# Attention, MoE and MLP in one static plan: the port of SBUF in the planner, routing on GpSimd, weight residues on VectorE, and the first pair split out of PSUM in pieces

## The chip, the cores and the metric

One core of a Trainium2 chip. The metric is the device time of one execution in microseconds (us), the median of the runs. Engines are named as in the profile: PE is TensorE (PEld its weight loads), DVE is VectorE, ACT is ScalarE, POOL is GpSimd, SP is SyncE, which here only issues DMAs.

## The reference

```python
def reference(q, k, v, moe_*, moe2_*):        # all float32
    x = attention(q, k, v)                    # [4, 8, 576, 64], block causal mask (blocks of 64), softmax
    x = x.transpose(0, 2, 1, 3).reshape(2304, 512)
    logits = x @ w_gate                       # 8 experts
    noisy = logits + log1p(exp(x @ w_noise)) * noise
    # top 2 of 8 per token, softmax over the two
    x = sum_k top2_w[k] * (relu(x @ w1[e_k]) @ w2[e_k])     # w1 [8, 512, 1024], w2 [8, 1024, 512]
    h = x @ w_in                              # [512, 2048]
    return (h * clip(h + 3, 0, 6) / 6) @ w_out
```

## The kernel before

Every large product is made of three: each operand is split into a high part (rounded to fp32r) and a low part (the residue), and hi*hi, hi*lo and lo*hi are summed in PSUM. So each operand costs a cast and a subtraction on some engine besides its load.

**Attention** works through 16 pairs of heads, four pairs to a batch. For a pair, TensorE transposes q and k (`prep`), the result goes to SBUF (`prep_out`: `qs`, `ks`) and is split into `qd` and `kt` (`q_hi`, `q_lo`, `k_hi`, `k_lo`); `qd` holds the two heads side by side with zeros between, set once by memsets. Six score units (`scores`) fill the PSUM tiles `sb`; VectorE takes the row maximum (`rowmax`), ScalarE the exponential (`expo`), TensorE transposes P (`ptrans`), which is split again (`pt_hi`, `pt_lo`), then come P times v (`av`), and a product with `iw` (`fin`) that turns the heads' outputs back and adds their share of the router's logits. `lsum` adds up the logits of a batch's four pairs, `lgm` brings them into token order.

**Routing** (`route`) of a batch is a chain of some fifty small instructions: softplus, the noisy logits, the top two (`top`, `ti`), one-hots (`oh`, `ohb`), positions by a triangular product (`pos`), and the lists of token ids by a product of ten one-hot selections (`sel`) with two tables (`rid`), `idm`. Batches 0 to 2 are routed during attention. After batch 2 two tiles of tokens of expert 0 are gathered early (`early_load`). The last batch is routed after attention, while TensorE computes expert 0 for the two early tiles; then its `ids` allow the gathers of the other three tiles (`load_x`), and the experts and the MLP run in a written-out order to the end.

**The order** of attention and of the hand-over comes from a list scheduler in the kernel's Python, `Plan`. `add(engines with costs, function, deps, priority, take, drop)` records an operation; `run` walks a model of time, gives each free engine the ready operation of lowest priority number, and emits it. Where an operation lists two engines, the first is preferred. `PR` holds the priorities and choices, found offline; `SELS`, `WLS` and `VHS` are choices that it indexes. `plan` orders attention, `plan2` the hand-over. Each engine executes what is emitted in that order, and waits where an operand is late. TensorE first does WARM0 matmuls on zeros.

In the kernel before: the memsets of `qd` stand on GpSimd (L612); pair 0 goes the way of the other pairs, with its splits on VectorE, ScalarE and GpSimd; all four loads of q and k of the first pairs are issued by SyncE; of the routing GpSimd has most small steps of batch 0 alone (`rp`: 1), the selections are VectorE's in all batches; the residues of expert 0's weights in the hand-over are GpSimd's (`WLS[2]`, L324).

Of the kernel before, what the change touches and what calls it, by code (L numbers as in the profile page):

```python
# [19 lines left out]
WARM0 = 9  # L20
# [12 lines left out]
WLS = ({"DVE": 1.14, "POOL": 2.4}, {"POOL": 2.4, "DVE": 1.14}, {"POOL": 2.4})  # L33
VHS = ({"POOL": 2.3}, {"DVE": 0.42}, {"POOL": 2.3, "DVE": 0.42}, {"DVE": 0.42, "POOL": 2.3}, {"ACT": 0.65, "DVE": 0.42})
PR = {'v': -0.45, 'prep': -10.04, 'step': -0.65, 'qk': -35.17, 'keep': 1, 'S': 0.31, 'max': -27.6, 'exp': -16.28, 'pt': 0.44, 'hi': 17.54, 'lo': -16.57, 'hid': True, 'av': 4.37, 'o': 10.18, 'od': True, 'inv': -4.2, 'fin': 13.84, 'x': -26.38, 'route': 27.64, 'rp': 1, 'route2': 10.65, 'xt': 12, 'eg': 537.67, 'ex': 466.81, 'ew': 2093.4, 'first': 0, 'sel': 2, 'vh': 0, 'wl': 2, 'wa': 8.24, 'wb': 12.71, 'h': -29.8, 's2': 0.04, 'vs': (0.29, -0.33, -1.3, 0.67, -3.03, -2.34), 'vpt': (7.17, 2.34, 0.89, -2.5, -6.05, 0.37, 1.12, 0.7000000000000001), 'vp': (0.79, -0.62), 'vf': (0.46, -1.86)}
# [10 lines left out]
class Plan:  # L46
# [11 lines left out]
    def add(self, eng, fn, deps=(), prio=0.0, take=None, drop=None, lat=None, after=0.0):  # L58
        if drop is not None:
            drop.left += 1  # L60
        self.ops.append((eng, fn, {d for d in deps if d is not None}, prio, take, drop, lat))
        self.ready.append(after)
        return len(self.ops) - 1

    def run(self, start):
# [10 lines left out]
        back = []  # L76
        left = len(ops)
        now = 0.0
        while left:
# [4 lines left out]
            for e in self.LAT:  # L84
# [3 lines left out]
                for i in open_:  # L88
# [13 lines left out]
                eng, fn, _, _, take, drop, lat = ops[i]  # L102
# [6 lines left out]
                free[e] = end  # L109
                done = end + (self.LAT[e] if lat is None else lat)  # L110
# [21 lines left out]
def kernel(  # L132
# [51 lines left out]
    def load(p, nm):  # L184
# [4 lines left out]
        for i in range(2):  # L189
            nc.sync.dma_start(t[:, 0:NC - 1, i], hs[i, 0:S - BLK, :].rearrange("(c p) d -> p c d", p=128))  # L190
        nc.sync.dma_start(t[:BLK, NC - 1], hs[:, S - BLK:, :].rearrange("h p d -> p h d"))

    for nm in "qk":
        nc.vector.memset(raw[nm, 0][64:, NC - 1], 0.0)
        load(0, nm)
# [154 lines left out]
    def early(shape, nm):  # L350
        return e_p.tile(shape, F32R, name=nm)
# [50 lines left out]
    def route(b, dep, add, bank, psum, prio0, after=0.0):  # L402
# [12 lines left out]
        def step(nm, eng, fn, *deps, **kw):  # L415
            prio[0] += 0.25
            dp[nm] = add(eng, fn, [dp[d] for d in deps] if deps else dep, prio[0], after=after, **kw)
# [3 lines left out]
        po = {"POOL": 0.3} if b < PR["rp"] else dv  # L421
# [770 lines left out]
    k2 = {}  # L1192
# [178 lines left out]
```

## Time and profile before

| | |
|---|---|
| median of 3 runs | 1132.49 us (1131.97 to 1132.53) |
| the profiled execution | 1132.54 us, of it 1130.8 us span |
| busy: TensorE, VectorE, ScalarE, GpSimd | 1106.3, 767.4, 525.9, 315.0 us |
| mean granted clock of TensorE | 0.987 |

TensorE's row of 40 slices (28 us each), in tenths: 7 in the first, 9 in nearly all others, 8 in the last. The granted clock is 7 in the first slice and 9 (90% or more) elsewhere. A granted clock of 1.00 is 2.4 GHz, 0.50 is 1.2 GHz; a mean between the two mixes stretches of both.

### The profile page before, as it was taken

How to read it: one execution, taken by the hardware profiler on the slowest of the kernel's cores; microseconds unless marked ns; L12 is line 12 of the kernel's file. 1: busy time of each engine (PE TensorE's matmuls, PEld its weight loads, DVE VectorE, ACT ScalarE, POOL GpSimd, SP SyncE). 2: the span in 40 equal slices, each digit the busy share in tenths (PEclk: the TensorE clock that was granted, in tenths of full speed). 3: DMA queues.
4: the chain of work that ended last, by engine and by line, in shares of the span. 5: the costliest groups of instructions: out<-in, count | busy, mean ns of one | idle time of the engine just before them, and what ended most of it. 6: DMA issues, size and time to landing. Idle time of an engine off the chain costs nothing. (4 is left out here: it accounts for less than half of the span.)

```text
span 1130.8 us, 17329 instructions
## 1 busy us (share of the span) xinstructions
PE 1106.3 (98%) x6426; PEld 981.4 (87%) x6426; DVE 767.4 (68%) x1432; ACT 525.9 (47%) x1074; POOL 315.0 (28%) x333
## 2 busy tenths in 40 slices
PE   7999999998999999999999999999999999999998
PEld 6999989897889999999999989898888888888886
DVE  6777897887577877887887865687554655554542
ACT  4877767653433333333333334565444444344442
POOL 7677776627401010101010000266220320200000
PEclk7999999998999999999999999999999999999999
DMA  5555442120977667567446323412101110000000
GB/s 121 140 125 125 91 104 64 23 60 15 334 271 274 213 236 268 205 225 241 164 165 219 136 101 111 152 47 75 47 28 38 46 30 38 19 1 1 38 1 38
DMA packets 141152, 130.82 MB, mean 116 GB/s; under 512 B 85768, under 2 KB 106248, under 8 KB 141064
## 3 DMA queue, kind: packets, MB, share of 16 engines
q1 hardware_dynamic: 127784, 100.30, 28.6%
q0 software_dynamic: 6080, 19.93, 6.0%
q10 hardware_dynamic: 7200, 9.44, 2.4%
q8 instruction: 52, 0.85, 0.3%
q14 instruction: 36, 0.29, 0.1%
HBM read 92.94 MB, written 36.70 MB: 115 GB/s over the span
## 5 line engine op out<-in xcount | busy, mean ns | idle before, releaser
L366 PE MATMUL h<-xh,wah 128*128 128x312 f32 (+5 forms) x832 | 280.5, 337 | 1.8 <-ACT xh L340 0.7
L367 PE MATMUL h<-xl,wah 128*128 128x312 f32 (+5 forms) x832 | 275.5, 331 | 0.3 <-DVE xl L345 0.3
L368 PE MATMUL h<-xh,wal 128*128 128x312 f32 (+5 forms) x832 | 275.4, 331 | 0.0
L1007 PE MATMUL y<-wbh,hh 128*128 128x512 f32 (+1 forms) x608 | 238.5, 392 | 2.2 <-issue 2.2
L1008 PE MATMUL y<-wbl,hh 128*128 128x512 f32 (+1 forms) x608 | 239.0, 393 | 0.0
L1009 PE MATMUL y<-wbh,hl 128*128 128x512 f32 (+1 forms) x608 | 238.1, 392 | 0.0
L366 PEld LDWEIGHTS h<-xh,wah 128*128 128x128 f32 x832 | 157.9, 190 | 14.4 <-DVE hl L392 0.9
L367 PEld LDWEIGHTS h<-xl,wah 128*128 128x128 f32 x832 | 158.0, 190 | 12.0 <-DVE xl L345 0.5
L368 PEld LDWEIGHTS h<-xh,wal 128*128 128x128 f32 x832 | 157.8, 190 | 10.3
L1009 PEld LDWEIGHTS y<-wbh,hl 128*128 128x128 f32 (+1 forms) x608 | 114.0, 187 | 25.4
L1007 PEld LDWEIGHTS y<-wbh,hh 128*128 128x128 f32 (+1 forms) x608 | 113.9, 187 | 24.1 <-issue 2.6
L1008 PEld LDWEIGHTS y<-wbl,hh 128*128 128x128 f32 (+1 forms) x608 | 113.9, 187 | 21.6
L1300 DVE SCALAR_TENSOR_TENSOR r<-r,h 128x512 f32<-128x512 f32 (+1 forms) x80 | 50.6, 633 | 109.5 <-ACT r L1299 109.2
L389 ACT ACTIVATE hh<-h 128x312 fp32r<-128x312 f32 (+4 forms) x128 | 55.1, 431 | 149.2 <-PE h L368 147.2
L1171 POOL DMA_INDIRECT ga<-y_tab,slot x32 | 37.2, 1162 | 293.4 <-DMA y_tab<-yo 112.1
L985 POOL DMA_INDIRECT xn<-x_tok,ids x38 | 38.5, 1013 | 269.1 <-PE xps L337 266.5
L1299 ACT ACTIVATE r<-h,three 128x512 f32<-128x512 f32 (+1 forms) x80 | 51.6, 645 | 127.5 <-PE h L368 127.4
L324 DVE TENSOR_TENSOR wal<-wa,wah 128x1024 fp32r<-128x1024 f32 x75 | 93.2, 1243 | 14.3 <-ACT wah L320 13.3
L324 DVE TENSOR_TENSOR wbl<-wb,wbh 128x1024 fp32r<-128x1024 f32 x71 | 86.6, 1220 | 13.4 <-ACT wbh L320 10.7
L722 ACT ACTIVATE P<-sb,nm 128x576 f32<-128x576 f32 (+4 forms) x144 | 75.4, 530 | 39.7 <-DVE nm L716 37.0
L320 ACT CAST wbh<-wb 128x1024 fp32r<-128x1024 f32 x80 | 84.0, 1050 | 17.7 <-PE y L1009 16.3
L340 ACT CAST xh<-xps 128x512 fp32r<-128x512 f32 x56 | 32.8, 587 | 127.4 <-PE xps L337 127.4
(246 smaller groups left out, 1871.3 us busy)
## 6 DMA issues: line engine op xcount, KB each, us to landing
wa<-in_moe_w_dram SPq DMA_DIRECT2D x23, 512.0 KB
wb<-in_moe_w_dram SPq DMA_DIRECT2D x23, 512.0 KB
y_tab<-yo SPq DMA_DIRECT2D x32, 256.0 KB
w<-in_moe_w_in_dram SPq DMA_DIRECT2D x16, 512.0 KB
y_tab<-zero SPq DMA_DIRECT2D x8, 1024.0 KB
w<-in_moe_w_out_dram SPq DMA_DIRECT2D x16, 512.0 KB
x_tok<-x SPq DMA_DIRECT2D x32, 144.0 KB
wa<-in_moe_w_dram ACTq DMA_DIRECT2D x9, 512.0 KB
```

The costliest lines, as they stand in the source:

```text
L320: nc.scalar.copy(w_s[which, u][0], raws[PS[u]][which])
L324: (nc.gpsimd if e == "POOL" else nc.vector).tensor_tensor(lo, raws[PS[u]][which], hi.bitcast(F32), op=OP.subtract)
L366: nc.tensor.matmul(ps, lhsT=wh, rhs=xh, start=first, stop=False)
L367: nc.tensor.matmul(ps, lhsT=wh, rhs=xl, start=False, stop=False)
L368: nc.tensor.matmul(ps, lhsT=wl, rhs=xh, start=False, stop=last)
L389: nc.scalar.activation(h[0][:, c0:c1], ps[:, :c1 - c0], AF.Relu)
L722: nc.scalar.activation(o, views.pop((p, i)), AF.Exp, bias=nms.pop((p, i)), scale=1.0, accum_out=rs[p % 3][:, i:i + 1])
L1007: nc.tensor.matmul(yps[t][:n], lhsT=hh[:, sl], rhs=wh[:, f % 2], start=first, stop=False)
L1008: nc.tensor.matmul(yps[t][:n], lhsT=hh[:, sl], rhs=wl[:, f % 2], start=False, stop=False)
L1009: nc.tensor.matmul(yps[t][:n], lhsT=hl[:, sl], rhs=wh[:, f % 2], start=False, stop=last)
L1299: nc.scalar.activation(r[:, :n], ps[:, :n], AF.Relu, bias=three, scale=1.0)
L1300: nc.vector.scalar_tensor_tensor(r[:, :n], r[:, :n], 6.0, ps[:, :n], op0=OP.min, op1=OP.mult)
```

## The change

- `Plan` gets a flag `port` per operation and a record `held`: a flagged operation of VectorE or GpSimd is not placed while the other of the two runs a flagged one. Splits from SBUF, sums of logits and most routing steps are flagged.
- `route`: for batches 0 to 2 all elementwise steps, the tables and the ten selections go to GpSimd (the fused step `nl0` becomes two); for the last batch all go to VectorE.
- Weight residues of expert 0 go to VectorE (`wl`: 0). Two units, (0, 0) and (1, 0), are split during attention (`PRE`), not one.
- Pair 0: k is loaded from ScalarE's queue; q and k are split straight out of PSUM in three pieces (`first_hi`, `first_lo`: blocks 0 to 3, 4 to 7, 8), and a score unit waits only for the pieces that it reads. The `qd` memsets go to VectorE. WARM0 is 6 for 9, and FILL = 8 matmuls on zeros may be placed where TensorE has nothing ready (lowest priority).
- `PR` is new throughout: the order of attention and of the hand-over changes everywhere.

```diff
-WARM0 = 9
+WARM0 = 6
+FILL = 8
+PRE = ((0, 0), (1, 0))
-WLS = ({"DVE": 1.14, "POOL": 2.4}, {"POOL": 2.4, "DVE": 1.14}, {"POOL": 2.4})
+WLS = ({"DVE": 1.2}, {"DVE": 1.14, "POOL": 2.4}, {"POOL": 2.4, "DVE": 1.14}, {"POOL": 2.4})
...
+                    if o[7] and e in other and held[other[e]] > now:
+                        continue
...
+                if port and e in other:
+                    held[e] = end
...
-        load(0, nm)
+        load(0, nm, nc.sync if nm == "q" else nc.scalar)
...
+            port = nm not in ("ez", "lu", "e2", "top", "ti", "pos", "t", "pi", "idm", "id", "os", "cnt", "short")
...
         off = {"DVE": 0.11} if last else {"POOL": 0.24}
-        po = {"POOL": 0.3} if b < PR["rp"] else dv
+        po = off
...
-                step(f"sel{i}{c}", ({"DVE": 0.17, "POOL": 0.6} if last else SELS[PR["sel"]]), lambda e, i=i, c=c: eng_of(e).tensor_scalar(
+                step(f"sel{i}{c}", ({"DVE": 0.17} if last else {"POOL": 0.61}), lambda e, i=i, c=c: eng_of(e).tensor_scalar(
...
-                    nc.gpsimd.memset(t[64 * h:64 * h + 64, :, 1 - h].bitcast(F32), 0.0)
+                    nc.vector.memset(t[64 * h:64 * h + 64, :, 1 - h].bitcast(F32), 0.0)
...
+        FIRST = ((0, 4), (4, 8), (8, NB))
+        def first_hi(e, g, nm, m):
+            src = first_src(g, nm, m)
+            i = slice(*FIRST[m])
+            if nm == "k":
+                copy(e, kt[0][0][:, i.start * BLK:i.stop * BLK], src)
+                return
+            for h in range(2):
+                r = slice(64 * h, 64 * h + 64)
+                scale(e, qd[0][0][r, i, h], src[r].rearrange("p (i s) -> p i s", s=BLK))
+        def first_lo(e, g, nm, m):
...
+            if nm == "k":
...
+                nc.vector.tensor_tensor(kt[0][1][:, c], src, kt[0][0][:, c].bitcast(F32), op=OP.subtract)
+                return
...
+                nc.vector.scalar_tensor_tensor(qd[0][1][r, i, h], src[r].rearrange("p (i s) -> p i s", s=BLK), qscale,
+                                               qd[0][0][r, i, h].bitcast(F32), op0=OP.mult, op1=OP.subtract)
...
+                for n_ in range(FILL):
+                    g = Bank("t", 1)
+                    add({"PE": 0.23}, lambda e, g=g: nc.tensor.matmul(tb[g.bank], lhsT=ones, rhs=filler, start=True, stop=True),
+                        [k["T", 0, 2]], 1e6, take=g, drop=g)
...
+        for n_, (w, u) in enumerate(PRE):
+            hi_ = add({"ACT": 0.95}, lambda e, w=w, u=u: split_hi(w, u, early), [], PR["ew"] + n_, after=205.0)
+            add({"DVE": 1.2}, lambda e, w=w, u=u: split_lo(w, u, e), [hi_], PR["ew"] + n_, port=True)
```

VectorE at the start, between its constants and its first row maxima (`nm<-sb`), before:

```order
L224 COPY iw<-ident 64x4x64 x2
L580 COPY ks<-tb_172 128x512
L580 COPY ks<-tb_173 128x64
L580 CAST qd0h<-qs 64x9x64 x2
L684 TENSOR_TENSOR qd0l<-qs,qd0h 64x9x64 x2
L251 CAST laneb<-lane 128x128
L252 CAST tidi<-tid 128x20
L253 TENSOR_SCALAR tidh<-tidi 128x20
L254 CAST tab<-tidh 128x20
L255 TENSOR_SCALAR tidi<-tidi 128x20
L256 CAST tab<-tidi 128x20
L580 CAST sp_v<-raw_v_77 128x10x64
```

and now:

```order
L234 COPY iw<-ident 64x4x64 x2
L630 MEMSET qd0h 64x9x64 x2
L630 MEMSET qd0l 64x9x64 x2
L630 MEMSET qd1h 64x9x64 x2
L630 MEMSET qd1l 64x9x64 x2
L733 SCALAR_TENSOR_TENSOR qd0l<-tb_171,qd0h 64x4x64 x2
L729 TENSOR_TENSOR kl<-tb_172,kh 128x256
L733 SCALAR_TENSOR_TENSOR qd0l<-tb_171,qd0h 64x4x64 x2
L729 TENSOR_TENSOR kl<-tb_172,kh 128x256
L733 SCALAR_TENSOR_TENSOR qd0l<-tb_173,qd0h 64x64 x2
L729 TENSOR_TENSOR kl<-tb_173,kh 128x64
L765 TENSOR_REDUCE nm<-sb_176 128x1 x3
```

The splits of pair 0 come from PSUM (`tb`) in pieces, behind eight memsets, and the six table operations (`laneb`, `tidi`, `tidh`, `tab`) stand further down. On TensorE, seven of the eight fillers stand between the transposes of pair 0 and its first score.

VectorE in the hand-over, from the copy of the last batch's logits (`lg`) on, before:

```order
L580 COPY lg_154<-tb_173 128x80
L432 TENSOR_SCALAR zc<-lg_154 128x40
L434 TENSOR_SCALAR zx<-lg_154 128x40
L427 TENSOR_TENSOR zx<-zx,noise 128x40
L427 TENSOR_TENSOR zx<-zx,lg_154 128x40
L436 TENSOR_SCALAR u<-ez 128x40
L427 TENSOR_TENSOR en<-ez,noise 128x40
L438 TENSOR_SCALAR dd<-u 128x40
L392 SCALAR_TENSOR_TENSOR hl<-h,hh 128x256
L440 RECIPROCAL rd<-dd 128x40
L427 TENSOR_TENSOR rd<-rd,en 128x40
```

and now (`wal`, `wbl` are the residues of expert 0's weights, `hl` that of its hidden layer):

```order
L598 COPY lg_154<-tb_173 128x80
L334 TENSOR_TENSOR wal<-wa,wah 128x1024
L446 TENSOR_SCALAR zc<-lg_154 128x40
L334 TENSOR_TENSOR wbl<-wb,wbh 128x1024
L448 TENSOR_SCALAR zx<-lg_154 128x40
L450 TENSOR_SCALAR u<-ez 128x40
L441 TENSOR_TENSOR en<-ez,noise 128x40
L441 TENSOR_TENSOR zx<-zx,noise 128x40
L452 TENSOR_SCALAR dd<-u 128x40
L405 SCALAR_TENSOR_TENSOR hl<-h,hh 128x256
L454 RECIPROCAL rd<-dd 128x40
L441 TENSOR_TENSOR zx<-zx,lg_154 128x40
```

Two weight residues stand within the first three routing steps; three more follow ahead of `ids`.

GpSimd at the end of attention, before the two early gathers (`raw_q`, `raw_k`), before:

```order
L427 TENSOR_TENSOR ohsum_138<-os,ohsum_137 128x8
L427 TENSOR_TENSOR bw_3389<-bt_3382,tab 128x50
L427 TENSOR_TENSOR bw_3395<-bt_3384,tab 128x50
L505 TENSOR_TENSOR rid_3401<-ohs_130,bw_3389 128x400
L505 TENSOR_TENSOR rid_3426<-ohs_130,bw_3395 128x400
L808 TENSOR_TENSOR lgp_220<-lgp_220,x 64x144 x2
L357 DMA raw_q_72<-x_tok,ids_155 128x512
L357 DMA raw_k_74<-x_tok,ids_155 128x512
```

and now:

```order
L523 TENSOR_TENSOR rid_3487<-ohs_130,bw_3421 128x400
L527 TENSOR_SCALAR sel_3498<-laneb,pmf 128x128
L527 TENSOR_SCALAR sel_3503<-laneb,pmf 128x128
L527 TENSOR_SCALAR sel_3511<-laneb,pmf 128x128
L857 TENSOR_TENSOR lgp_220<-lgp_220,x 64x144 x2
L527 TENSOR_SCALAR sel_3535<-laneb,pmf 128x128
L527 TENSOR_SCALAR sel_3540<-laneb,pmf 128x128
L667 TENSOR_TENSOR sp_v<-raw_v_77,sp_v 128x10x64
L370 DMA raw_q_72<-x_tok,ids_155 128x512
L370 DMA raw_k_74<-x_tok,ids_155 128x512
```

The last five of the ten selections of batch 2, and the low part of the last pair's v (`sp_v`), stand ahead of the gathers.

## Rows read from the trace of the kernel before

**Rows 1.** Busy time by stage: us, busy of TensorE, its loads, VectorE, ScalarE, GpSimd; granted clock

```profile
0.00:24.00 24.00, 17.55 (x74) 13.58 (x75) 15.28 (x33) 9.74 (x26) 20.09 (x44) 0.72 0.61 136
24.00:250.00 226.00, 220.27 (x1772) 211.93 (x1771) 180.99 (x480) 162.93 (x513) 146.97 (x182) 0.99 0.39 90
250.00:287.00 37.00, 31.47 (x197) 27.59 (x196) 28.49 (x76) 15.85 (x27) 25.72 (x15) 0.91 0.19 50
287.00:1130.80 843.80, 836.97 (x4389) 728.34 (x4388) 542.66 (x845) 337.41 (x509) 122.22 (x93) 1.00 0.37 125
```

**Rows 2.** The same view, one stretch of the fill

```profile
10.00:22.00 12.00, 10.35 (x42) 8.87 (x43) 8.88 (x16) 5.16 (x18) 11.37 (x10) 0.50 0.70 159
```

**Rows 3.** Instructions of TensorE in order of time: start, us, [idle before]

```profile
1.98 4.00 PE L636 MATMUL tb<-filler,ones 128*128 128x512 bf16 x9 [1.98 <-DVE filler L204]
...
5.77 0.66 PE L658 MATMUL tb<-ident,raw_q 128*128 128x128 f32 x4
...
13.05 0.40 PE L708 MATMUL sb<-kh,qd0h 128*128 128x64 f32 x1
...
27.75 0.28 PE L708 MATMUL sb<-kh,qd1h 128*128 128x64 f32 x1
```

**Rows 4.** The same view, VectorE at the start

```profile
1.65 0.27 DVE L204 MEMSET filler<- 128x256 uint32 x1
...
2.16 0.29 DVE L224 COPY iw<-ident 64x256 f32<-64x256 f32 x1
...
9.31 3.91 DVE L684 TENSOR_TENSOR qd0l<-qs,qd0h 64x576 fp32r<-64x576 f32 x2
...
16.93 0.41 DVE L716 TENSOR_REDUCE nm<-sb 128x1 f32<-128x64 f32 x2
```

**Rows 5.** The same view, VectorE in the hand-over

```profile
253.82 0.23 DVE L580 COPY lg<-tb 128x80 f32<-128x80 f32 x1
...
256.23 2.31 DVE L427 TENSOR_TENSOR zx<-zx,lg 128x40 f32<-128x40 f32 x1
...
258.55 0.19 DVE L427 TENSOR_TENSOR en<-ez,noise 128x40 f32<-128x40 f32 x1
...
267.07 0.25 DVE L509 TENSOR_SCALAR sel<-laneb,pmf 128x128 bf16<-128x128 bf16 x1
...
268.03 6.38 DVE L509 TENSOR_SCALAR sel<-laneb,pmf 128x128 bf16<-128x128 bf16 x8
...
277.88 1.19 DVE L530 SCALAR_TENSOR_TENSOR ids<-idacc 128x40 int32<-128x40 f32 x1
...
291.70 1.23 DVE L324 TENSOR_TENSOR wbl<-wb,wbh 128x1024 fp32r<-128x1024 f32 x1 [1.09 <-issue]
```

**Rows 6.** The same view, GpSimd at both places

```profile
18.35 1.40 POOL L692 TENSOR_TENSOR kl<-ks,kh 128x576 fp32r<-128x576 f32 x1
...
246.15 0.94 POOL L357 DMA_INDIRECT raw_k<-x_tok,ids  x1 [0.30 <-issue]
...
250.09 0.49 POOL L808 TENSOR_TENSOR lgp<-lgp,x 64x144 f32<-64x144 f32 x1 [2.44 <-DMA raw_k<-x_tok,ids]
...
256.08 2.40 POOL L324 TENSOR_TENSOR wbl<-wb,wbh 128x1024 fp32r<-128x1024 f32 x1
...
291.47 0.95 POOL L985 DMA_INDIRECT xn<-x_tok,ids  x1 [0.30 <-issue]
```

**Rows 7.** The same view, TensorE at the end of the hand-over

```profile
286.69 0.44 PE L366 MATMUL h<-xh,wah 128*128 128x368 f32 x1 [0.67 <-ACT xh L340]
```

**Rows 8.** The same view, an evacuation and a residue of 256 columns

```profile
20.52 0.39 ACT L580 CAST pth<-tb 128x256 fp32r<-128x256 f32 x1
...
22.09 0.41 DVE L755 TENSOR_TENSOR ptl<-tb,pth 128x256 fp32r<-128x256 f32 x1
```

**Rows 9.** Busy time of one batch, then GpSimd's groups: count, busy us, mean ns

```profile
70.00:130.00 60.00, 60.00 (x490) 59.10 (x489) 44.77 (x115) 45.93 (x149) 44.35 (x55) 1.00 0.46 107
...
L1183 POOL TENSOR_SCALAR ga<-ga,rw 128x512 f32<-128x512 f32 x14 | 28.0, 2011 | 0.4
```

More of the change, by code (lines that the diff above doesn't have):

```diff
@@ L56, in __init__, with add @@
         self.pools = {p: list(range(n)) for p, n in pools.items()}
-    def add(self, eng, fn, deps=(), prio=0.0, take=None, drop=None, lat=None, after=0.0):
+    def add(self, eng, fn, deps=(), prio=0.0, take=None, drop=None, lat=None, after=0.0, port=False):
         if drop is not None:
             drop.left += 1
-        self.ops.append((eng, fn, {d for d in deps if d is not None}, prio, take, drop, lat))
+        self.ops.append((eng, fn, {d for d in deps if d is not None}, prio, take, drop, lat, port))
         self.ready.append(after)
@@ L76, in run @@
         back = []
+        held = {"DVE": 0.0, "POOL": 0.0}
+        other = {"DVE": "POOL", "POOL": "DVE"}
         left = len(ops)
@@ L101, in run @@
                 i = best[1]
-                eng, fn, _, _, take, drop, lat = ops[i]
+                eng, fn, _, _, take, drop, lat, port = ops[i]
                 if take is not None:
@@ L182, with load @@
     k_in, k = k, {}
-    def load(p, nm):
+    def load(p, nm, queue=None):
+        queue = queue or nc.sync
         src = {"q": q, "k": k_in, "v": v}[nm]
@@ L350, in early @@
     def early(shape, nm):
-        return e_p.tile(shape, F32R, name=nm)
+        early.n += 1
+        return e_p.tile(shape, F32R, name=f"{nm}{early.n}")
+    early.n = 0
     xn = {}
@@ L499, in route @@
             G = [128, NC, NT, 2]
-            tts(f"bw{i}", {"DVE": 0.13} if last and i == 0 else {"POOL": 0.3}, new(f"bw{i}", G, BF16),
+            tts(f"bw{i}", {"DVE": 0.13} if last else {"POOL": 0.24}, new(f"bw{i}", G, BF16),
                 lambda i=i: T[f"bt{i}"][:, :, :, None].to_broadcast(G),
@@ L504, in route @@
             Q = [128, NC, E, 2 * NT]
-            step(f"rid{i}", {"DVE": 0.49} if last and i == 0 else {"POOL": 1.0}, lambda e, i=i: eng_of(e).tensor_tensor(
+            step(f"rid{i}", {"DVE": 0.49} if last else {"POOL": 0.82}, lambda e, i=i: eng_of(e).tensor_tensor(
                 tl(f"rid{i}", Q, BF16), oh[:, i, :, :, None].to_broadcast(Q),
@@ L836, in s_cost @@
             return 3 * (max(0.11, L / 2400.0 + 0.0135) if L <= 512 else 2 * (L / 4800.0 + 0.0135))
-        k["tab"] = add({"DVE": 0.9}, lambda e: tables(), [], 3, after=12.0)
+        k["tab"] = add({"DVE": 0.9}, lambda e: tables(), [], 3, after=12.0, port=True)
         for p in range(NPAIR):
@@ L855 @@
             k["hi", p] = add({"DVE": 0.42, "ACT": 0.65} if p < 2 else VHS[PR["vh"]], lambda e, p=p: hi(e, p),
-                             [k["L", "v", p]] + [k.get(("AV", p - 3, h, r)) for h in range(2) for r in range(2)], vu)
-            k["lo", p] = add({"POOL": 1.5}, lambda e, p=p: lo(e, p), [k["hi", p]], vu)
+                             [k["L", "v", p]] + [k.get(("AV", p - 3, h, r)) for h in range(2) for r in range(2)], vu, port=True)
+            k["lo", p] = add({"POOL": 1.52}, lambda e, p=p: lo(e, p), [k["hi", p]], vu, port=True)
             outs = {}
@@ L879 @@
             for u in range(NU):
+                if p == 0:
+                    ready = [k[n_, 0, m] for n_ in ("qh", "ql", "kh", "kl") for m in range(1 + sum(max(UN[u]) >= FIRST[i][0] for i in (1, 2)))]
                 U = u0 + u + PR["vs"][u]
@@ L1208, in wops @@
     def wops(which, u, deps, prio):
+        if (which, u) in PRE:
+            return None
         hi = add({"ACT": 0.95}, lambda e: split_hi(which, u), deps, prio)
-        return add(WLS[PR["wl"]], lambda e: split_lo(which, u, e), [hi], prio)
+        return add(WLS[PR["wl"]], lambda e: split_lo(which, u, e), [hi], prio, port=True)
     n_ = AHEAD * 128
```

76 lines of the change are left out of this document (49 added, 27 removed).

## The prediction

> **What bounds the kernel now.** I read the busy time by stage first. TensorE is busy for 836.97 of the last 843.80 us and for 220.27 of the 226 us of steady attention; only the first 24 us (17.55 busy) and the 37 us in which attention hands over to the experts (31.47 busy) have holes [rows 1]. The diff touches nothing that runs after the hand-over, so the last stage should keep its length and start earlier or later as a block. The question is how much of the idle 6.45 + 5.73 + 5.53 us goes, and how much of the time at the low clock: in the middle of the fill TensorE was busy for 10.35 of 12 us at a granted clock of 0.50 (the 1.2 GHz level) [rows 2], and the hand-over's mean of 0.91 [rows 1] means that some 0.18 of its 37 us, 6.7 us, ran at that level. Such a stretch is "busy" and still costs about half its length.
>
> Next the order of time at the start. Nine warm-up matmuls end at 5.98, the transposes of pair 0 follow at 5.77, and the first score matmul waits until 13.05, after a stretch with little work, over which the clock fell [rows 3, 2]. What it waited for is VectorE's low part of q: two instructions, 3.91 us, ending at 13.22 (the second score matmul does not read it, so the two overlap a little) [rows 4]. Then VectorE did its six table operations and a copy of v, and the first row maximum came only at 16.93 [rows 4].
>
> Then the hand-over. Between the copy of the last logits at 253.82 and the expert ids at 277.88 + 1.19 = 279.07, VectorE walks the routing of the last batch, 25.25 us for some fifty small instructions [rows 5]. One of them, 128x40, took 2.31 us, while another of the same size took 0.19 [rows 5]. The long ones lie beside GpSimd's 2.40 us weight splits [rows 6]: the 2.31 us one began 0.15 us after such a split and ended as it ended. TensorE began expert 0's remaining tiles at 286.69, 7.6 us after the ids [rows 7].
>
> **The change part by part: the start.** VectorE is free at 2.16 + 0.29 = 2.45 [rows 4]. It now gets the eight 64x576 memsets. A memset of 256 words took it 0.27 us [rows 4], so one costs 0.61 at the same rate; eight end at about 7.3. This is on the path, and I count it. On TensorE, six warm-ups instead of nine end at 1.98 + 6 x 0.444 = 4.65 [rows 3]. q had landed by 5.77 at the latest; k, issued in parallel from ScalarE's queue, shares the engines with it, so I put both at 5.0, between those bounds. Four transposes take 0.66 at the high level and twice that at the low one [rows 3]: q is in PSUM by 5.7 to 6.3. ScalarE makes piece 0 in three casts of 256 columns, 0.39 each [rows 8], done by 7.5 at the latest, its issue of three loads and the table load lying before 5. VectorE follows with three of 0.41 [rows 8]: 7.3 + 1.2 = 8.5. The first score can go at 8.6, **4.4 us earlier**. VectorE then does piece 1 (three of 0.41) and piece 2 (three of 64 columns, some 0.2 each) and reaches the first row maximum at 10.4 instead of 16.93, **6.5 us earlier**, since the tables now stand behind it in VectorE's order. That is what the whole softmax chain hangs on, and I take 6.5. Low end 3.5: the score's 4.4 less a microsecond of queueing. High end 9: some of the low-clock time goes too, if the eight fillers keep TensorE from falling; the fillers themselves lie where it had nothing to do. What is late next is pair 1: its last split on GpSimd ended at 18.35 + 1.40 = 19.75 and its first score ran at 27.75 [rows 6, 3]. 6.5 us earlier that is 21.25, so the slack shrinks from 8 us to 1.5 even if GpSimd gains nothing; it is rid of the eight memsets, and SyncE's queue loses the three loads of k, so q and k of pair 1 are issued sooner.
>
> **The hand-over.** Four single instructions of the chain ran 1.78, 2.31, 1.06 and 2.23 us (the row of 2.31 stands for them), against 0.19: 6.6 us too long. Eight selections took 6.38 where the first took 0.25 [rows 5]: 4.4 more. The ids instruction took 1.19 instead of some 0.2. That is 12.0 us which goes with GpSimd's splits. Against it the order puts five weight splits on VectorE ahead of the ids, at 1.23 each [rows 5], 6.2 us, and a second table product and id product, 0.8. The ids come 12.0 - 7.0 = **5.0 us earlier**, and the three gathers and expert 0 with them. TensorE has the work of the two early tiles meanwhile, and could give up at most 5.53 idle + half of the 6.7 at the low clock = 8.9 [rows 1]. Low end 2: each residue of h (0.4 us) now queues behind a split, and second-layer matmuls wait for it.
>
> At the gathers a rule speaks against the move. The row shows a gather issued at 291.47 taking 0.95 while a 1.23 us VectorE split began beside it [rows 6, 5], no longer than its neighbours. The Trainium skill (SBUF — State Buffer, section "SBUF: two separate sides") says that a VectorE instruction in a mode which uses both its ports keeps GpSimd from writing a gather's descriptors; the same page takes two-operand instructions out of this, by inference alone. By the row the gathers cost nothing more; by the rule three of them could each wait for a split, 3 x 1.23 less the microsecond of slack that they have, and the forecast would be some 2.5 us higher.
>
> **Steady attention.** Here TensorE idles 5.73 us in all [rows 1], so no order of the work can win more. Moving the routing of batches 0 to 2 to GpSimd frees VectorE, which was no bound. At its end one new thing hangs on GpSimd: its last selections of batch 2 now stand just ahead of the low part of the last v and of the two early gathers. The second gather was issued at 246.15 and had landed by 250.09 [rows 6]; 3.9 us from issue, plus the two before it, is about the 6 us of TensorE work left behind the id product, so up to 1 us may show. I take a gain of 1.0, between +5.7 and -5. The two early splits of unit 0 on VectorE (2.5 us) lie in a stage where it idles a fifth of the time, and cost nothing unless the row maxima queue behind them.
>
> **Sum.** 6.5 + 5.0 + 1.0 = 12.5 us. The profiled execution took 1132.54, so 1120.0; the median of the runs is 0.05 lower, which changes nothing.
>
> **The rivals.** *GpSimd becomes the bound of attention*, and the kernel slower. For four pairs, one batch, GpSimd was busy 44.35 of 60 us [rows 9]. Ten selections at 0.50 each (a quarter of the 2.01 us that a 128x512 instruction of this form takes it [rows 9]) and some thirteen small ones at up to 0.36 add 9.7: 54 of 60. It decides from 60 on, when splits of q and k come late. If its 23 small ones are drawn out as VectorE's were, to 1.0 us each, it needs 67; three batches are then 22 us late, and with 11.5 won elsewhere the time is 1143. For it: nine tenths full, in a fixed order. Against it: its splits are due well after they are made, pair 1's last one 8 us [rows 6, 3]. The Trainium skill (same page, section "Who interferes with whom") lets only those VectorE instructions collide that use the second port, and counts those with at most one operand in SBUF out; by that rule the row maxima and the P residues, which read PSUM, would not draw GpSimd out, and no row here shows them doing so. Chance 0.08.
>
> *The clock stays low through the fill.* With three warm-ups fewer, TensorE may still be at 1.2 GHz when the scores start, and what VectorE gives, it loses: the start wins 3.5, the time is 1123. For it: the low clock held for 12 us before [rows 2]. Chance 0.15.
>
> *VectorE fills up in the hand-over.* It was busy 28.49 of 37 us there [rows 1]; 11 us of drawn-out time leave and about 11 us of splits arrive. If they stand in the way of h, the stage wins 2 instead of 5: 1123. Chance 0.15.
>
> *The new order does not do what its planner says.* All priorities are new, and the middle could lose 5 us in new waits for P or for GpSimd's batch 2: 1126. Chance 0.10.
>
> **How the numbers follow.** The forecast, within a few microseconds of 1120, has 0.52. The range of 1112.5 to 1129 takes in the three milder rivals and, on the low side, 7.5 of the 11.1 us that the three stages could give beyond my values (2.5 + 3.9 + 4.7), since they will hardly all go to their ends at once; the GpSimd rival stays outside with the tails. About 0.2% (2.3 us) is what a measurement of this kernel tells from no change. Faster by more: 0.52 + 0.15 + 0.15 and 0.06 of the last rival, 0.88. Within: the other 0.04. Slower: 0.08.
>
> **What would show it.** In the profile after: the first score near 8.6 and the first row maximum near 10.4; pair 1's first score near 21; in the routing of the last batch no 128x40 instruction over 0.5 us and ids some 20 us after the logits; expert 0's first matmul 12 to 13 us before 286.69; the last stage as long as before. I am wrong if VectorE's memsets run far longer than 0.61, if the first score is early and pair 1's is not, or if GpSimd's busy share in a batch passes nine tenths and TensorE waits for its splits.

## The result, and the profile after

The changed kernel takes 1120.64 us (median of 4 runs, 1119.02 to 1122.26) against 1132.23 us (4 runs, 1131.16 to 1132.53): a ratio of 0.9899, 95% interval 0.9881 to 0.9918. The forecast was 1120.0. The execution that was profiled took 1119.59 us with a span of 1117.8, 13.0 us below the profiled one of before. Here are the stages of its busy time, in the columns of [rows 1]; the last stage begins at expert 0's first matmul:

```profile
0.00:24.00 24.00, 20.23 (x115) 16.23 (x116) 18.66 (x49) 13.46 (x41) 13.10 (x37) 0.93 0.63 137
24.00:250.00 226.00, 219.10 (x1764) 209.96 (x1763) 166.58 (x429) 169.11 (x513) 172.15 (x239) 1.00 0.40 92
...
275.69:1117.80 842.11, 835.74 (x4389) 727.93 (x4389) 542.92 (x845) 337.63 (x509) 118.03 (x88) 1.00 0.37 125
```

In the middle some 14 us of VectorE's work are gone and 25 us of GpSimd's have come, and TensorE is as busy as before. I divide the 13.0 us by four points in time, from the instructions of TensorE and of VectorE. First the fill. TensorE's first score, its second, and pair 1's first score, in order of time [rows 3]:

```profile
8.52 0.38 PE L757 MATMUL sb<-kh,qd0h 128*128 128x64 f32 x1
10.61 0.30 PE L757 MATMUL sb<-kl,qd0h 128*128 128x64 f32 x1 [1.71 <-DVE kl L729]
...
23.01 0.28 PE L757 MATMUL sb<-kh,qd1h 128*128 128x64 f32 x1
```

The same view for VectorE, with the first memset, the first low part of q and of k, and the first row maximum [rows 4]:

```profile
2.61 0.54 DVE L630 MEMSET qd0h<- 64x576 f32 x1 [0.16 <-issue]
...
8.05 0.86 DVE L733 SCALAR_TENSOR_TENSOR qd0l<-tb,qd0h 64x256 fp32r<-64x256 f32 x2
10.13 0.42 DVE L729 TENSOR_TENSOR kl<-tb,kh 128x256 fp32r<-128x256 f32 x1 [1.22 <-ACT kh L598]
...
12.28 0.42 DVE L765 TENSOR_REDUCE nm<-sb 128x1 f32<-128x64 f32 x2
```

And for ScalarE, which makes the high parts:

```profile
5.65 0.77 ACT L602 ACTIVATE qd0h<-tb 64x256 fp32r<-64x256 f32 x2 [1.78 <-PE tb L677]
6.50 0.37 ACT L598 CAST kh<-tb 128x256 fp32r<-128x256 f32 x1
8.94 0.77 ACT L602 ACTIVATE qd0h<-tb 64x256 fp32r<-64x256 f32 x2 [2.07 <-DVE qd0l L733]
```

The first score went 4.53 us earlier than at 13.05, the first row maximum 4.65 earlier than at 16.93, pair 1's first score 4.74 earlier than at 27.75. But the two engines hand the pieces back and forth: ScalarE waits 2.07 us for VectorE's low part of q, and VectorE then 1.22 us for ScalarE's next high part of k, though its own first low part of k needs only the high part that was there by 6.9.

Next the hand-over, VectorE in order of time [rows 5]:

```profile
249.12 0.23 DVE L598 COPY lg<-tb 128x80 f32<-128x80 f32 x1
249.27 1.21 DVE L334 TENSOR_TENSOR wal<-wa,wah 128x1024 fp32r<-128x1024 f32 x1
...
251.83 0.20 DVE L441 TENSOR_TENSOR en<-ez,noise 128x40 f32<-128x40 f32 x1
...
261.90 0.90 DVE L527 TENSOR_SCALAR sel<-laneb,pmf 128x128 bf16<-128x128 bf16 x5
...
264.73 0.20 DVE L548 SCALAR_TENSOR_TENSOR ids<-idacc 128x40 int32<-128x40 f32 x1
```

No instruction of the routing is drawn out: five selections take 0.90 us where eight took 6.38, the ids 0.20 instead of 1.19. The ids are there 15.81 us after the start of the logits' copy (264.93 less 249.12), where it had been 25.25. TensorE's first matmul of expert 0 [rows 7]:

```profile
275.69 0.44 PE L379 MATMUL h<-xh,wah 128*128 128x368 f32 x1 [0.73 <-ACT xh L350]
```

| stage | before, us | after, us | won, us |
|---|---|---|---|
| to pair 1's first score | 27.75 | 23.01 | 4.74 |
| on to the last batch's logits | 226.07 | 226.11 | -0.04 |
| on to expert 0's first matmul | 32.87 | 26.57 | 6.30 |
| the last stage | 844.11 | 842.11 | 2.00 |

### The profile page after: what moved, and what is told of

It reads as the page before. It is cut to its first block, busy times and chain, and to the rows that moved or that the text cites. A ratio compares the mean times of both kernels' runs of the same rounds, so it can differ in the third digit from the quotient of the medians.

```text
span 1117.8 us, 17336 instructions
## 1 busy us (share of the span) xinstructions
PE 1099.4 (98%) x6431; PEld 975.4 (87%) x6431; DVE 749.0 (67%) x1397; ACT 531.8 (48%) x1083; POOL 311.1 (28%) x370
## 5 line engine op out<-in xcount | busy, mean ns | idle before, releaser
L380 PEld LDWEIGHTS h<-xl,wah 128*128 128x128 f32 x832 | 157.2, 189 | 12.5 <-DVE xl L355 1.0
L334 DVE TENSOR_TENSOR wal<-wa,wah 128x1024 fp32r<-128x1024 f32 x80 | 99.3, 1241 | 15.5 <-ACT wah L330 14.7
L334 DVE TENSOR_TENSOR wbl<-wb,wbh 128x1024 fp32r<-128x1024 f32 x76 | 92.7, 1220 | 15.0 <-ACT wbh L330 15.0
L1371 DVE TENSOR_TENSOR hl<-r,hh 128x512 fp32r<-128x512 f32 (+1 forms) x80 | 56.4, 705 | 51.5 <-ACT hh L1370 51.5
L771 ACT ACTIVATE P<-sb,nm 128x64 f32<-128x64 f32 (+6 forms) x144 | 75.4, 530 | 31.2 <-DVE nm L765 29.9
```

The lines of the kernel that those rows point to most:

```text
L334: (nc.gpsimd if e == "POOL" else nc.vector).tensor_tensor(lo, raws[PS[u]][which], hi.bitcast(F32), op=OP.subtract)
L380: nc.tensor.matmul(ps, lhsT=wh, rhs=xl, start=False, stop=False)
L771: nc.scalar.activation(o, views.pop((p, i)), AF.Exp, bias=nms.pop((p, i)), scale=1.0, accum_out=rs[p % 3][:, i:i + 1])
L1371: nc.vector.tensor_tensor(hl[:, :n], r[:, :n], hh[:, :n].bitcast(F32), op=OP.subtract)
```

## The experiments

**The start: who waits for whom.** Run 1 issues the first pair's low parts behind ScalarE's first four high parts, so that the program, and with it the order in which the two engines read a PSUM bank, no longer puts a low part between two high ones:

```
         def first_lo(e, g, nm, m):
+            if not first_lo.open:
+                held_lo.append(lambda: first_lo_(e, g, nm, m))
+                return
...
+            if (nm, m) == ("k", 1):
+                first_lo.open = True
+                flush_lo()
```

> Edit: pair 0's low parts are written down after ScalarE's first four high parts, in the same order on every engine. In the changed kernel ScalarE's second q piece starts at 8.94, when VectorE's first low part of q ends, and VectorE's first low part of k starts only at 10.13, when ScalarE's second k piece ends; the theory is that reads of one PSUM bank by two engines are put in the order in which they are written down. Theory A (that ordering costs the start 1.2 us): ScalarE runs its pieces through by 8.7, first low part of k ends near 9.4 instead of 10.55, first row maximum near 11.1 instead of 12.28, pair 1's first score near 21.9 instead of 23.01, span some 1.1 us shorter. Theory B (the splits of pair 1 on GpSimd or its loads set the pace from there on): row maximum 11.1, but pair 1's first score stays at 22.8 to 23.2 and the span too. Theory C (another wait, not the banks): the first low part of k still ends at 10.5.

Its VectorE and ScalarE in the same stretch, in order of time, VectorE's two lines first:

```profile
8.06 0.86 DVE L753 SCALAR_TENSOR_TENSOR qd0l<-tb,qd0h 64x256 fp32r<-64x256 f32 x2
8.95 0.42 DVE L749 TENSOR_TENSOR kl<-tb,kh 128x256 fp32r<-128x256 f32 x1
...
6.44 0.37 ACT L598 CAST kh<-tb 128x256 fp32r<-128x256 f32 x1
6.70 0.77 ACT L602 ACTIVATE qd0h<-tb 64x256 fp32r<-64x256 f32 x2
...
7.76 0.45 ACT L602 ACTIVATE qd0h<-tb 64x64 fp32r<-64x64 f32 x2
```

Both waits are gone. The first row maximum comes at 11.09 instead of 12.28, pair 1's first score at 21.41 instead of 23.01, expert 0's first matmul at 274.05 instead of 275.69. The dependence between the engines cost 1.2 us at the row maximum. Of the 1.6 us at pair 1 some 0.4 are the clock's: in the changed kernel's profile it was low from 11 to 14.4 us and in run 1 it was not, and in the three profiles with the changed start in which it was not (runs 4, 9 and 10) pair 1's first score came at 22.60 to 22.61. Against these, run 1 is 1.2 us earlier at pair 1 too. It fell in the changed kernel's profile and in runs 5 and 7, and in none of the four with moved low parts or memsets (runs 1, 2, 3 and 8); whether the edits keep it up is not shown. That the wait is for the bank, and not for the tile `qd0h` that both engines touch, is seen in run 1: ScalarE wrote its third piece of `qd0h`, which comes from another bank, at 7.76, ahead of VectorE's first low part at 8.06, which stands before it in the program and reads the same tile. The time was 1119.44: the last stage took 843.55 us, not 842.11, which is taken up below.

Runs 2 and 3 give the memsets back to GpSimd, run 2 by itself and run 3 together with the edit of run 1:

```
-                    nc.vector.memset(t[64 * h:64 * h + 64, :, 1 - h].bitcast(F32), 0.0)
+                    nc.gpsimd.memset(t[64 * h:64 * h + 64, :, 1 - h].bitcast(F32), 0.0)
```

> Edit: the eight memsets of qd go back to GpSimd, nothing else. In the changed kernel VectorE's memsets come at 0.70 us each and end at 8.04; the first low part of q starts at 8.05 though its high part is done at 6.42. Theory A (the memsets hold the first pair): the first low part of q starts near 6.5, first row maximum near 10.7, pair 1's first score near 21.5, span 1.5 us shorter. Theory B (pair 1's splits set the pace): row maximum 10.7, pair 1's first score within 0.3 of 23.0, span unchanged. GpSimd's first other operation comes at 11.4, so its own order should not be late.

> Edit: both of the two before. Theory A (either alone takes the wait off, and the reads of one bank are in series in both): first low part of q near 7.6, behind ScalarE's first four pieces, first row maximum near 10.6, as with the memsets alone. Theory B (the two gains add): row maximum near 9.5.

| | after | memsets back | both |
|---|---|---|---|
| first low part of q | 8.05 | 6.38 | 7.50 |
| first row maximum | 12.28 | 10.60 | 10.54 |
| pair 1's first score | 23.01 | 20.91 | 20.85 |
| last batch's logits | 249.12 | 247.78 | 247.64 |
| expert 0's first matmul | 275.69 | 274.22 | 273.94 |
| time | 1119.59 | 1119.72 | 1119.39 |

So the memsets were on the path as well, but the two gains don't add: run 3 ends where run 2 ends. Against run 10 (22.61 at pair 1, 248.58 at the logits, the clock up in the fill as in runs 2 and 3) the memsets' move wins 1.7 us at the start, as at the row maximum, and 0.8 of it is left at the logits; what takes the rest I did not find. The times do not show the gains, because the last stage took 843.6 us in runs 2 and 3, for a reason that comes below.

**The fillers.** Run 6 issues none of the eight.

```
-                    add({"PE": 0.23}, lambda e, g=g: nc.tensor.matmul(tb[g.bank], lhsT=ones, rhs=filler, start=True, stop=True),
+                    add({"PE": 0.23}, lambda e: None,
```

> The changed kernel, with the eight filler matmuls that the change puts between the pieces of the first pair not issued. Nothing else is moved. Theory A (the low clock at 11.0 to 14.4 us comes after TensorE's idle stretch of 9 to 10.6 us, which the fillers, all but one of them run before 8.9 us, don't fill): the fillers hold nothing up and keep nothing fast at the place where it counts; with them gone TensorE is idle from about 7.1 us, the clock falls earlier, up to 2 us earlier, and is granted in full again at 12.5 to 14.5 us; pair 1's first score at 22.3 to 23.2 us. Theory B (the fillers keep the clock up): low until well past 14.4 us, pair 1's first score at 23.8 to 26 us, expert 0's first matmul 0.8 to 3 us later than 275.69. Theory C (they cost nothing and give nothing): low at 11.0 to 14.4 us, pair 1 at 23.0 within 0.2.

Busy time by stretch, first without the fillers, then of the changed kernel (the granted clock is the third number from the end):

```profile
9.00:10.00 1.00, 0.00 (x0) 0.00 (x0) 0.00 (x0) 0.98 (x3) 0.00 (x0) 0.57 0.52 120
10.00:11.00 1.00, 0.38 (x2) 0.39 (x3) 0.85 (x3) 0.98 (x5) 0.00 (x0) 0.50 0.85 191
...
15.00:16.00 1.00, 1.00 (x7) 1.00 (x6) 0.75 (x2) 0.57 (x4) 0.26 (x1) 0.52 0.80 183
```

```profile
9.00:11.00 2.00, 0.39 (x4) 0.40 (x4) 0.86 (x3) 1.95 (x7) 0.00 (x0) 1.00 0.67 153
11.00:12.00 1.00, 1.00 (x7) 1.00 (x7) 0.97 (x4) 0.29 (x1) 0.58 (x1) 0.56 0.64 146
...
15.00:16.00 1.00, 1.00 (x8) 0.84 (x7) 0.33 (x1) 0.92 (x5) 0.63 (x1) 1.00 0.71 163
```

Without the fillers the clock fell to its lower level (0.50) between 9 and 10 us and was back only after 15; with them it fell at 11 and was back before 15. Pair 1's first score came at 23.57, expert 0's at 276.73, 1.04 later than in the changed kernel. By the place of the fall theory A held, by its length and its price B, at a smaller size than B gave. In the second profile of the changed kernel (run 10) the clock stayed at 1.00 from 8 to 17 us, and pair 1 began at 22.61, and in run 5, with the same start, the clock fell as in the first profile and pair 1 began at 23.09. So the fillers are worth 0.5 to 1.0 us here, from a single profile without them (time 1122.10).

**The hand-over.** Run 4 does the change's weight splits on GpSimd, at the same places, and nothing else.

```
-        return add(WLS[PR["wl"]], lambda e: split_lo(which, u, e), [hi], prio, port=True)
+        return add(WLS[PR["wl"]], lambda e: split_lo(which, u, "POOL"), [hi], prio, port=True)
```

> Edit: in the hand-over the weight residues run on GpSimd again, at the same places of the written order. Theory A (a GpSimd subtraction from SBUF to SBUF draws out VectorE's small two-operand instructions beside it): 128x40 instructions of 1 to 2.4 us come back in the routing of the last batch, the selections take more than 4 us instead of 1.9, ids end 6 to 10 us later than 15.8 us after the logits, expert 0's first matmul 4 to 6 us later than 26.6 us after the logits, span 4 to 6 us longer. Theory B (VectorE's relief came from the new order, not from the engine of the residues): ids 3 to 5 us earlier than in the changed kernel, since 6 us of splits leave VectorE, and expert 0 no later than 26.6.

Here are GpSimd's splits, and then VectorE's routing beside them, in order of time:

```profile
250.94 2.39 POOL L334 TENSOR_TENSOR wbl<-wb,wbh 128x1024 fp32r<-128x1024 f32 x1
253.31 2.39 POOL L334 TENSOR_TENSOR wal<-wa,wah 128x1024 fp32r<-128x1024 f32 x1
255.66 2.36 POOL L334 TENSOR_TENSOR wbl<-wb,wbh 128x1024 fp32r<-128x1024 f32 x1
```

```profile
251.01 2.38 DVE L441 TENSOR_TENSOR en<-ez,noise 128x40 f32<-128x40 f32 x1
...
253.42 2.33 DVE L452 TENSOR_SCALAR dd<-u 128x40 f32<-128x40 f32 x1
255.66 0.41 DVE L405 SCALAR_TENSOR_TENSOR hl<-h,hh 128x256 fp32r<-128x256 f32 x1
...
256.31 1.78 DVE L441 TENSOR_TENSOR zx<-zx,lg 128x40 f32<-128x40 f32 x1
...
264.61 2.42 DVE L527 TENSOR_SCALAR sel<-laneb,pmf 128x128 bf16<-128x128 bf16 x1
```

The product of 128x40 that takes 0.20 us in the changed kernel takes 2.38 and ends 0.06 us after the split beside it; two more go the same way, to within 0.07 us of the next splits' ends, and so does the first of the ten selections, beside a fifth split (264.54, 2.44 us). The residue of h, which reads one of its operands from PSUM, took 0.41 while a split ran beside it, as it does alone. The ids came 6.1 us later (21.88 behind the logits), and the gathers, each now behind a split on GpSimd, 3.5 us apart instead of 1.77 and 1.26; expert 0's first matmul came 33.8 us after the logits, 7.2 more than in the changed kernel. TensorE in this stage of run 4, and its longest wait there:

```profile
248.60:282.40 33.80, 27.50 (x171) 23.34 (x171) 21.17 (x71) 12.61 (x23) 22.91 (x12) 0.95 0.13 36
...
PE y L1075 <- DVE hl L405: 3.9, 1, 3.9
```

It waited 3.9 us for the residue of h that stood behind the drawn-out steps, until 255.66, and the clock was low for part of 256 to 260 us behind that wait; for gathers it waited 1.5 us instead of 0.6. Its idle time is 6.30 us instead of 1.48 (below), and the same work took 27.50 us at a mean clock of 0.95 instead of 25.12 at 1.00: 4.8 and 2.4 make the 7.2. The 4 to 6 us that I expected left the clock and the gathers' queue out. Time 1126.2. With the splits back on GpSimd the whole gain of this stage, 6.30, is gone.

**The middle.** This stage gave nothing; the question is which gains and losses make up the zero. Run 5 gives the first three batches' routing to VectorE again, at the places that the plan had chosen for GpSimd; run 9 lets the planner place it anew for VectorE; the products `bw` and `rid` stay on GpSimd in both. Run 7 plans without the rule on the shared port. Parts of the edits of run 5, run 9 and run 7, in this order:

```
         def eng_of(e):
-            return nc.gpsimd if e == "POOL" else nc.vector
+            return nc.vector
...
-        po = off
+        po = dv
...
-({"DVE": 0.17} if last else {"POOL": 0.61})
+({"DVE": 0.17} if last else {"DVE": 0.17, "POOL": 0.61})
...
-                    if o[7] and e in other and held[other[e]] > now:
-                        continue
```

> The changed kernel, with the routing steps of the first three batches (all but the two that make row numbers and weight offsets) given to VectorE again, at the same places in the order; the last batch and the weight splits stay as changed. Theory A (the middle, from pair 1's first score to the last batch's logits, is set by TensorE's order; GpSimd or VectorE has room enough for this routing): pair 1's first score stays at 23.0 us, the logits come 225.5 to 227.5 us behind it (226.1 in the changed kernel), expert 0's first matmul is at 275 to 277.5, VectorE's busy time from 24 to 250 us rises from 166.6 towards the 181.0 of before and GpSimd's falls from 172 towards 147. Theory B (taking the routing off VectorE gained in the middle what the new order lost there, so that the two cancelled): the logits come 2 to 5 us later, at 228 to 231 us behind pair 1, and the span is 1120 to 1123.

> The changed kernel, with the first three batches' routing planned for VectorE as before the change (the first batch's too, which before had on GpSimd; row numbers and weight offsets stay on GpSimd, the selections where the plan likes), all priorities as changed, and the order planned anew: the fair form of the run that moved the same steps without a new plan and came 8.1 us later at the logits. Theory A (most of those 8.1 us came of places chosen for the other engine): pair 1's first score at 23.0, the logits 226 to 229 us behind it (226.1 in the changed kernel, 226.1 before the change), span 1117 to 1121. Theory B (with this order's priorities VectorE, behind which TensorE waits for P's low parts and the row maxima's exponentials, can't carry the routing: GpSimd's taking it is worth what the rest of the new order costs): the logits 230 to 235 us behind, span 1122 to 1128.

> The changed kernel, planned without the rule that holds an operation of GpSimd or VectorE back while the plan has the other at work in an operation that takes the shared port; all engines, costs and priorities stay. Theory A (the rule in the plan changes the order but no wait that TensorE sees in the middle): pair 1's first score at 22.5 to 23.5 us, the logits 225.5 to 227.5 us behind it (226.1), expert 0's first matmul at 274.5 to 277, span within 2.2 us of 1117.8. Theory B (without the rule the planned times are wrong by the drawn-out operations and the order fits the chip less well): the logits 2 to 6 us later, the span 1120 to 1124.

Busy time from pair 1's first score to the last batch's logits: run 5, run 9, and the changed kernel in run 10, one fence each:

```profile
23.09:257.30 234.21, 224.03 (x1767) 213.20 (x1765) 183.72 (x511) 168.99 (x513) 140.70 (x160) 0.99 0.38 88
```

```profile
22.61:250.47 227.86, 219.31 (x1768) 209.94 (x1767) 184.52 (x498) 168.15 (x514) 144.96 (x173) 1.00 0.40 90
```

```profile
22.61:248.58 225.97, 219.49 (x1767) 210.11 (x1765) 166.61 (x430) 168.56 (x512) 173.26 (x241) 1.00 0.40 91
```

With the places kept, the routing on VectorE costs 8.1 us (234.21 against 226.11 in the first profile), more than either theory gave (time 1129.51): TensorE idles 3.4 us more, its waits for P and for the selections grow, and it works 224 us instead of 219, with a mean clock of 0.99 where the changed kernel has 1.00; the clock was low in run 5 for most of 246 to 254 us. With a new plan 1.9 us are left (time 1122.23). So theory A of run 9 holds: most of run 5's loss is the old places'. Run 7's logits came 227.77 us after pair 1's first score (23.45 to 251.22), 1.7 more than the 226.11, just outside theory A's bounds; its time was 1123.34. Each of the two prices comes from one profile; in the eight profiles whose middle is planned as in the changed kernel the stage took 225.97 to 226.87 us, so the routing's move is worth 1 to 2 us in the middle with these priorities, and the rule as much. What takes the two gains away again was not tried by itself; the priorities are all new, and the two prices may not add. The waits of TensorE from 24 to 250 us say where to look: those for P's low parts on VectorE fell from 2.3 to 1.0 us, but those for P on ScalarE grew from 2.1 to 4.3, and 0.6 for GpSimd came new. The clock hides more: in the kernel before it was low around 206 to 212 us (a mean of 0.73 from 205 to 210) and in the changed kernel nowhere in the middle, and the stage is no shorter for it.

**The last stage.** Nothing in the change touches it, and still it was 2.0 us shorter. In both kernels TensorE idles 2.2 us in one place, at the loop over the overflow tiles (for tokens that an expert's own tiles have no room for). Busy time by stretch around it, before the change and after:

```profile
719.00:721.00 2.00, 1.12 (x5) 0.52 (x3) 1.54 (x2) 0.23 (x1) 0.00 (x0) 1.00 0.00 0
721.00:723.00 2.00, 0.68 (x2) 0.61 (x3) 0.00 (x0) 0.00 (x0) 0.00 (x0) 0.92 0.05 12
723.00:725.00 2.00, 2.00 (x7) 1.46 (x6) 0.00 (x0) 1.26 (x2) 0.00 (x0) 0.50 0.00 0
725.00:727.00 2.00, 2.00 (x14) 2.00 (x14) 1.82 (x2) 0.27 (x1) 0.00 (x0) 0.73 0.54 188
```

```profile
708.00:710.00 2.00, 1.14 (x5) 0.54 (x4) 1.54 (x2) 0.26 (x1) 0.00 (x0) 1.00 0.02 4
710.00:712.00 2.00, 0.66 (x3) 0.57 (x4) 0.00 (x0) 0.00 (x0) 0.00 (x0) 1.00 0.05 12
712.00:714.00 2.00, 2.00 (x15) 1.79 (x14) 0.79 (x2) 1.53 (x2) 0.00 (x0) 1.00 0.10 38
```

The idle time is the same; in the one the clock fell behind it, in the other it did not. Run 8 (the kernel of run 1) and run 10 (the changed kernel, unaltered) were each executed several times beside the kernel before:

> The changed kernel with the first pair's low parts issued behind ScalarE's first four high parts (the first of these runs), timed in rounds. Theory A (the 1.6 us that it gains at the start stay; the clock at the overflow loop's idle of 2.2 us falls in some executions and not in others, worth 2.0 us, with it as without): times in two groups 1.5 to 2.5 us apart, about 1117.5 and 1119.5, median 1117.5 to 1119.5, ratio to the kernel before 0.987 to 0.989. Theory B (the gain at the start is given back later in the last stage because the work there comes earlier, as the one look's 843.5 us suggests): one group at 1119 to 1120 with no run under 1118.5, the same as the changed kernel's own lower group.

> The changed kernel itself, unaltered, in rounds beside the kernel before. Theory A (the 2.0 us that the last stage was shorter in the profiled execution are the clock's, which falls at the overflow loop's idle in some executions of either kernel and not in others): both kernels show two groups of times, the changed one about 1119.3 and 1122.0, the one before about 1130.0 and 1132.8; group against group the difference is 10.3 to 11.3 us, which is the first matmul of expert 0 coming 11.0 us earlier. Theory B (the changed last stage is itself shorter by 2 us): the changed kernel has one group near 1119.5, and its difference to the lower group of before is 10.5, to the upper 13.

Run 10's times were 1119.02, 1119.61, 1120.77 and 1120.85 us, median 1120.19, ratio 0.9896 (0.9879 to 0.9912); its profile shows the clock at 1.00 at this place. Run 8's were 1118.20, 1118.23, 1118.58, 1119.57 and 1120.73, median 1118.58, ratio 0.9892 (0.9875 to 0.9909); its profile shows no fall either, and a last stage of 842.2. Over all profiles, the last stage took 841.9 to 842.2 us where the clock held (the changed kernel, runs 4, 8 and 10) and 843.5 to 844.1 where it fell (before, and runs 1, 2, 3, 5, 6, 7 and 9). That is A in its main point: the same program does both (runs 1 and 8 are one kernel), and the last stage's 1.4 to 2.0 us over the changed kernel's 842.11 are the clock's. The groups were not as clean as A said: run 10's lie 1.5 us apart rather than 2.7, and the kernel before gave 1129.76 to 1133.21 in 9 runs beside run 8, but 1130.94 to 1132.70 in 7 beside run 10. B, by which the gain at the start is given back, falls with run 8's 1118.2.

Run 8 is the best version that I have: its expert 0 starts 1.5 us earlier than in the changed kernel's first profile and 0.9 earlier than in its second. The two ratios' intervals overlap, so the times alone do not set it apart.

## Why the prediction was right, point by point

- **The start, 6.5: it gave 4.74**, within the bounds of 3.5 and 9. Two terms were off. The memsets took 0.54 us each, less than my 0.61, but followed each other every 0.70, so that the first low part of q began at 8.05 and not at 7.3 (0.75). And I let VectorE and ScalarE work side by side on one piece each, where the order in which they read a bank cost 1.22 us more (run 1). The first row maximum came at 12.28 instead of 10.4, which is about these two. That the start's gain is that of the first row maximum was right: 4.65 and 4.74, though 0.4 more hangs on the clock (run 10, where it stayed up in the fill, began pair 1 at 22.61, 5.14 earlier than before). That the first score came at 8.52, near my 8.6, is luck: seven fillers stood ahead of it, without them (run 6) it ran at 6.80, and the second score, which needs the low part of k, came at 10.61 with them and at 10.62 without. I also had four transposes at the lower clock take twice 0.66 us; in the kernel before they took 1.09 there (from 9.90 on).
- **The memsets at a price of their own** was right as a mechanism: with them off VectorE the row maximum came 1.7 us earlier (run 2).
- **The hand-over, 5.0: it gave 6.30.** The step that was mis-sized is "12.0 - 7.0". The five splits cost what I said (6.1 us). But VectorE's whole time from the logits to the ids fell by 9.44: 7.57 less busy (22.62 to 15.05) and 1.87 less idle (2.63 to 0.76), since the ids had also stood behind a residue of h that waited 2.21 us for ScalarE. I had counted only the drawn-out instructions, and low: the ten selections fell from 6.90 to 1.88 us, and five residues of h stand ahead of the ids where seven had. VectorE's time from the logits to the ids, before and after, and that residue between the two:

```profile
253.82:279.07 25.25, 21.73 (x139) 19.75 (x140) 22.62 (x64) 9.96 (x18) 18.12 (x9) 0.86 0.04 8
...
277.28 0.43 DVE L392 SCALAR_TENSOR_TENSOR hl<-h,hh 128x256 fp32r<-128x256 f32 x1 [2.21 <-ACT hh L389]
...
249.12:264.93 15.81, 15.67 (x114) 14.04 (x115) 15.05 (x70) 7.77 (x15) 0.00 (x0) 1.00 0.07 15
```

  Of the 9.44 only 6.30 reached expert 0, because TensorE is now the bound there. From the logits to expert 0's first matmul, before and after:

```profile
253.80:286.70 32.90, 28.36 (x173) 24.98 (x173) 25.07 (x69) 13.29 (x24) 24.88 (x14) 0.90 0.17 48
```

```profile
249.10:275.70 26.60, 25.12 (x172) 22.06 (x172) 21.76 (x79) 12.46 (x23) 7.85 (x7) 1.00 0.25 62
```

  Idle time fell from 4.54 to 1.48 us, and the same matmuls took 25.12 us at the full clock instead of 28.36 at 0.90: 3.06 + 3.24 = 6.30. The clock's row of before has an 8 for this stretch (254 to 283 us), its tenth slice, and not the 9 that I read there. With one profile of the kernel before, how much of the 3.24 comes in every execution is not shown.
- **The gathers.** The row of before showed no longer gather beside a split, and I took no cost. Here two of the first three were drawn out:

```profile
265.75 1.47 POOL L1051 DMA_INDIRECT xn<-x_tok,ids  x1 [22.40 <-ACT wah L330]
267.52 0.95 POOL L1051 DMA_INDIRECT xn<-x_tok,ids  x1 [0.30 <-issue]
268.78 1.65 POOL L1051 DMA_INDIRECT xn<-x_tok,ids  x1 [0.30 <-issue]
```

  VectorE's splits ran at 265.18, 266.31 and 268.38, 1.21 to 1.23 us each. The first gather began 0.64 us before the end of the first split, the third 0.83 before the end of the last, and they took 0.52 and 0.70 more than 0.95, the same within 0.01 in run 10. The second began as a split ended and took 0.95. In run 4, whose splits here are GpSimd's, the first five took 0.95 to 0.97; a later one that began 0.67 us before the end of a split of VectorE's took 1.49. And in the kernel before, a gather that began together with such a split, at 287.70, took 0.96. TensorE waited 0.6 us for a gather in this stage, so the price is at most that. The Trainium skill (SBUF — State Buffer, section "SBUF: two separate sides") says that a VectorE operation in a two-port mode shuts GpSimd out of writing descriptors, and its section "Who interferes with whom" takes two-operand instructions out by inference. The trace does not bear that inference out for these splits: a gather that begins while one runs comes late by what is left of it, less some 0.13 us, and one that begins with it or ahead of it does not.
- **GpSimd as the bound**, the rival on the slower side, did not come: GpSimd was busy 172.15 of 226 us, and 49.81 of 60 in its fullest stretch (70 to 130 us), where I had worked out 54. TensorE's waits in the middle are mostly for P on ScalarE and its low parts on VectorE; 0.6 us are for GpSimd's last selections and the last v's low part, of the up to 1 us that I had allowed. The rule that I cited there (the Trainium skill, SBUF — State Buffer, section "Who interferes with whom") is borne out by run 4: with two operands in SBUF 0.20 became 2.38 us, with one in PSUM it stayed 0.41. But `dd`, with one operand, in SBUF, went from 0.18 to 2.33: I had left out that the Trainium skill, in the same section, exempts such instructions only outside the two-port modes.
- **The clock in the fill**, a rival: it fell in the profiled execution for 3.4 us in place of 12, and in run 10 not at all; pair 1 began 0.4 us earlier there. The rival's 3 us were too much.
- **The middle, 1.0: it gave nothing.** Moving the routing "frees VectorE, which was no bound" was wrong as an argument: with these priorities it is worth up to 1.9 us (run 9), the plan's rule up to 1.7 (run 7), and something else in the new order, which I had as a rival of 5 us, takes that back; what, stays open.
- **The last stage, "as long as before"**: 2.0 us shorter in this execution, by the clock, as shown above. Without it the three stages sum to 11.0 where I had 12.5, against 11.6 between the medians. That the time came within 0.7 us of the 1120.0 is luck in part: the start gave 1.8 us less than I had and the middle 1.0 less, the hand-over 1.3 more, and the last stage's 2.0 were not forecast at all.

## What to carry to other kernels

When two engines share the drain of one PSUM bank, look at the order in which the program names their reads: here a low part that is written between two high parts made both engines wait, and moving lines alone took 1.2 us off the start. A shared-port lock is priced by whole chains: count the idle time behind the drawn-out instructions too, and then ask which engine has the next hole, since here only two thirds of the ids' gain reached the experts. Before a microsecond or two is put down to an edit, split the difference by stages and see whether one that the edit does not touch has changed as well.

## What the runs showed that I had not expected

- One idle stretch of 2.1 to 2.2 us, in every profile, was followed by a fall of TensorE's clock to 1.2 GHz in 8 of 12 profiles and not in the other 4, one program doing both; 1.4 to 2.0 us hang on it. In the fill the clock behaves likewise: with the same start it fell in the changed kernel's first profile and in run 5 and not in runs 4, 9 and 10, and pair 1 began 0.4 to 0.5 us later where it fell.
- In run 1 VectorE's 64x576 memsets still came with a hole of 0.16 us ahead of each, as in the changed kernel: a price per instruction of 0.70 us where the row says 0.54.
- VectorE's and ScalarE's reads of one PSUM bank wait for each other in the order in which the program issues them. The Trainium skill (PSUM — Partial Sum Buffer, section "PSUM bank collisions raise a hardware error") says that the hardware does not arbitrate such accesses and that software must keep two engines off one bank and quadrant. The waits of 2.07 and 1.22 us are how that looks in a trace here; what happens when two engines do read one bank together no run here shows.
